# An attention and feed-forward kernel whose engine queues are ordered by a planner: due times in place of keys written by hand, another order of the opening, larger weight pieces, two raw V buffers

## The chip, the cores and the metric

The kernel runs on one core of one Trainium2 chip. The metric is the device time of one execution in microseconds; the time before is 560.06 us, the median of three runs. The work of a core is done by five queues that run beside each other and wait for each other through semaphores: TensorE (PE: matmuls), VectorE (DVE), ScalarE (ACT), GpSimd (POOL), and SyncE (SP), which here issues all loads, transposes and copies by DMA; stores of the output are issued by ScalarE. Each queue is worked off in the order in which the program emits it, so an instruction that waits holds up all that stand behind it on its engine.

## The reference, cut to what matters

```python
# batch, n_heads, seq, head_dim = 8, 8, 576, 64;  d_model 512, d_ff 1024;  stride = 32
scores = scale * np.matmul(q, k.transpose(0, 1, 3, 2))
rel = pos[:, None] - pos[None, :]
mask_local = (rel >= 0) & (rel < stride)                       # heads 0 to 3
mask_strided = (rel >= 0) & (pos[None, :] % stride == pos[:, None] % stride)   # heads 4 to 7
attn = softmax(np.where(masks, scores, -1e9))                  # + 1e-9 in the denominator
x = (attn @ v).transpose(0, 2, 1, 3).reshape(B * S, H * D)     # 4608 x 512

h = x @ w_in
sm = softmax(h)                                                # + 1e-9 in the denominator
solu = h * sm
ln = (solu - mean(solu)) / np.sqrt(var(solu) + 1e-06) * g_ln
out = ln @ w_out
```

Half of the heads attend to the last 32 positions, the other half to positions of the same residue modulo 32. w_in and w_out arrive as float64.

## The kernel before, in words

**Tiling.** Attention is cut into 40 units, five for each of the 8 batches (`UNITS`): two strided units (6 and 5 groups of three residues, 54 positions each) and three local ones (3 blocks of 64 queries against 96 keys). The feed-forward part is cut into 36 tiles of 128 tokens (`ff`). A batch has 4.5 tiles, so one tile in nine lies across the boundary of two batches. The attention output goes to `xhi` and `xlo`, a ring of two batches, split into a high and a low float16 part; the feed-forward part multiplies three pairs (hi hi, hi lo, lo hi) in place of one fp32 product.

**A unit** (`unit`): scores on TensorE with the mask added by a matmul with the unit matrix (lines 342 and 347, into `s_ps`); row maximum and subtraction on VectorE (353, 354), exp on ScalarE (356), row sums and reciprocals on VectorE (357, 361, 362), scaling on GpSimd (365), high part on ScalarE (371) and low part on VectorE (372), a DMA transpose into `pt` (374), the product with V on TensorE (395, called pv, into `x_ps`), and its high and low parts into the ring (411, 412).

**V** (`load_v`, `v_scale`, `v_split`): each batch's V is loaded raw into one pair of buffers, `vrl` (local heads) and `vrs` (strided heads). ScalarE sums its squares (284); a matmul with a matrix of ones adds them over the partitions (249, `pow2_scale`); VectorE makes a power of two of it; V is split into two float16 parts (302, 303), and DMA copies bring them into the layouts `ve` and `vd` (318). The sum of the squares goes into the last column of the second bank of `s_ps`, the tile that the scores also write, and its step comes ahead of unit 0 in the plan.

**Weights** (`decode`, `prep_w`, `prep_o`): float64 values are loaded as pairs of 32-bit words, in 16 pieces of 512 KB (529), into "rooms": `e`, `u` and four `room` tiles for w_in, then `room`, one `ct` tile, `e[1]` and `u[1]` for w_out. ScalarE unpacks the high word (532), VectorE puts in the remaining bits (535, 536). Sums of squares (548, 561) give a scale through `pow2_scale`; then high and low float16 parts are made (553, 554 for w_in; 584, 586, 587 for w_out, after eight matmuls at 571 that subtract the mean over the gains).

**A tile** (`ff`): g1 is 24 matmuls of 512 columns in two halves of one PSUM bank each (453 to 455, into `h_ps`, three banks in turn). VectorE takes the maximum (460), ScalarE the exp (462), VectorE the product u and its sum (464), ScalarE the squares (468), GpSimd the two factors r and f (472 to 485); ScalarE and VectorE write the high and low parts of c = u r (492, 493); a DMA transpose makes `ct` of it (496); g2 is 24 matmuls into `o_ps` (505 to 507); ScalarE scales by f and stores (513). `e`, `u` and `c` have two buffers, `ct` has three. The factors r and f come from one GpSimd step that also needs the scale of w_out.

**What sets the order.** Nothing is issued directly. Each step is added to a `Plan` with its engine, an estimated duration, a function that emits it, a key, and what it reads and writes. `Plan.order` then simulates the five queues with these durations: whenever an engine is free, it takes, of the steps whose inputs are there, the one with the smallest key; the program is emitted in the order in which the simulation starts the steps. Semaphores enforce the dependencies on the chip, so the plan only fixes the order on each queue. The keys are hand-written numbers: `UK` for units, `TK` for tiles, `VK` and `LK` for V and loads, `LF` and `LW` for the first loads and the weights, with offsets within a unit or tile (`key + 0.35`):

```python
UK = [-40.0, -39.5, -39.0, -8.0, -7.0, *(n - 6.0 for n in range(5, B * NU))]
TK = [-6.5, -6.2, -5.9, *(1.11 * t + 1.0 - 2.0 * (t >= NT - 3) for t in range(3, NT))]
...
add("pe", 2.6, lambda i=i: g2(i), key + G2LAG, r=[(*CT, i, 0), (*CT, i, 1), *(("o_w", cc) for cc in range(4 * i, 4 * i + 4))], w=[O])
...
n = min((n for n in ns if ready_at[n] <= now), key=lambda n: (steps[n][3], n))
```

Of the kernel before, what the change touches and what calls it, by code (L numbers as in the profile page):

```python
# [61 lines left out]

class Plan:
# [29 lines left out]

    def order(self):
        steps = self.steps
        left = [len(s[4]) for s in steps]
# [45 lines left out]
def attn_solu_kernel(ctx: ExitStack, tc: tile.TileContext, qloc, qstr, kloc, kstr, vloc, vstr, w_in, w_out, g, masks, out):  # L142
# [67 lines left out]
    add("dve", 0.2, init, -9, w=["nhalf"])  # L210
    add("dve", 0.3, lambda: nc.vector.memset(ones, 1.0), -9, w=["ones"])

    def masks_bf16():
# [1 line left out]
        nc.vector.tensor_copy(mk_loc[:, 0, 0:1], m[:, 0:1])
# [2 lines left out]
        nc.vector.tensor_copy(mk_str, m[:, 2:3, 0:QS].broadcast_to([P, 6, QS]))
# [465 lines left out]
```

## Time and profile before

| | |
|---|---|
| three runs | 557.83, 560.06, 561.62 us; median 560.06 |
| profiled execution | span 558.1 us |
| TensorE busy | 483.2 us, 87% of the span |
| VectorE, ScalarE, GpSimd busy | 367.5, 298.2, 162.7 us |
| DMA | 96.90 MB, 174 GB/s in the mean; read from HBM 39.24 MB, written 9.44 MB |

The span is that of one profiled execution on the chip; the median of the runs lies 2.0 us above it. Engines overlap, so their busy times don't add up to the span. In the slices of the page each digit is the busy share of a fortieth of the span (14 us) in tenths; PEclk is the clock that TensorE was granted, in tenths of the full one. In a line of waits stand who waited, for whom, the total in us, how often, and the longest. In a line of the timeline stand start and duration in us, engine, line, operation, operands and number, and in brackets the idle time before it and what ended it. In a line of a group the number after "x" is the count, then busy us and mean ns of one, then the idle time before.

### The profile page before, as it was taken

Reading aid. Unit: us, or ns where it says so; the run is one execution under the profiler, and the core shown is the slowest. Engines: PE = TensorE matmul, PEld = TensorE weight load, DVE = VectorE, ACT = ScalarE, POOL = GpSimd, SP = SyncE. Lnnn points to the kernel's source line nnn. Section 1 sums busy time; section 2 is a strip of 40 time slices with the busy share of each in tenths; the row PEclk is TensorE's granted clock in tenths of the full one; section 3 lists DMA queues with packets and bytes.
Section 4 is the critical chain, followed back from the end, with each engine's and each line's share of the span. In section 5 each row is a group of like instructions: output and inputs, shape, how many; then the busy total and the mean of one; then the engine's idle time right before and its main releaser. Section 6 shows DMA issues by size and latency. Waiting matters only on the chain.

```text
span 558.1 us, 11783 instructions
## 1 busy us (share of the span) xinstructions
PE 483.2 (87%) x4808; PEld 249.6 (45%) x4808; DVE 367.5 (66%) x647; ACT 298.2 (53%) x440; POOL 162.7 (29%) x306
## 2 busy tenths in 40 slices
PE   0235875798969999999989999999999999999986
PEld 0232452355534555454545555545544554444432
DVE  3499588788865687695757857867566776342440
ACT  3783645375456367455465557546745545344360
POOL 2221004532333242242324332423404323123130
PEclk9999997699988999999999999999999999999999
DMA  8999396569994999599839996798669545542242
GB/s 312 413 282 217 94 213 160 125 135 209 249 210 86 233 254 174 101 230 239 200 66 208 200 252 156 168 275 177 147 95 229 129 96 111 83 95 75 58 111 78
DMA packets 171350, 96.90 MB, mean 174 GB/s; under 512 B 138400, under 2 KB 157472, under 8 KB 171296
## 3 DMA queue, kind: packets, MB, share of 16 engines
q1 hardware_dynamic: 166112, 86.71, 71.3%
q10 hardware_dynamic: 5184, 9.44, 5.3%
q8 instruction: 37, 0.61, 0.5%
q14 instruction: 17, 0.14, 0.1%
HBM read 39.24 MB, written 9.44 MB: 87 GB/s over the span
## 4 chain that ended last, share of the span: by engine, by line
PE 63%; DVE 15%; DMA 8%; ACT 5%; issue 4%; POOL 4%; SPq 0%; ACTq 0%; DVEq 0%; POOLq 0%
PE h_ps L453 10%; PE h_ps L455 9%; PE h_ps L454 9%; PE o_ps L505 8%; PE o_ps L507 7%; PE o_ps L506 7%; DMA vrl<-vloc 4%; PE x_ps L395 3%; PE s_ps L347 3%; DVE u L464 3%; DVE c L493 2%; DVE st L460 2%; DMA pt<-p 2%; PE o_ps L571 1%; DVE m L357 1%
## 5 line engine op out<-in xcount | busy, mean ns | idle before, releaser
L453 PE MATMUL h_ps<-w,xhi 128*128 128x512 f16 x280 | 109.3, 390 | 23.5 <-DVE u L464 18.8
L454 PE MATMUL h_ps<-w,xhi 128*128 128x512 f16 x280 | 109.0, 389 | 0.0
L455 PE MATMUL h_ps<-w,xlo 128*128 128x512 f16 x280 | 108.9, 389 | 0.0
L505 PE MATMUL o_ps<-obuf,ct 128*128 128x512 f16 x272 | 103.5, 381 | 0.8 <-ACT ob L513 0.8
L506 PE MATMUL o_ps<-obuf,ct 128*128 128x512 f16 x272 | 103.2, 379 | 0.0
L507 PE MATMUL o_ps<-obuf,ct 128*128 128x512 f16 x272 | 103.1, 379 | 0.0
L365 POOL TENSOR_TENSOR t<-t,m 128x576 f32<-128x576 f32 (+2 forms) x40 | 51.4, 1284 | 137.0 <-DVE m L362 93.1
L462 ACT ACTIVATE e<-h_ps,st,vsc 128x1024 f32<-128x1024 f32 x31 | 37.3, 1204 | 69.3 <-DVE st L461 51.5
L460 DVE TENSOR_REDUCE st<-h_ps 128x1 f32<-128x1024 f32 x35 | 42.7, 1220 | 43.6 <-PE h_ps L455 43.6
L472 POOL TENSOR_SCALAR st<-st 128x1 f32<-128x1 f32 x36 | 12.9, 358 | 174.7 <-DVE st L467 174.4
L464 DVE SCALAR_TENSOR_TENSOR u<-h_ps,e 128x1024 f32<-128x1024 f32 x35 | 42.7, 1221 | 28.3 <-ACT e L462 17.9
L493 DVE SCALAR_TENSOR_TENSOR c<-u,st,c 128x1024 f16<-128x1024 f32 (+1 forms) x38 | 48.1, 1271 | 13.0 <-ACT c L492 12.9
L492 ACT ACTIVATE c<-u,st 128x1024 f16<-128x1024 f32 (+1 forms) x38 | 41.6, 1100 | 26.3 <-POOL st L482 26.0
L468 ACT ACTIVATE e<-u,st 128x1024 f32<-128x1024 f32 x36 | 41.3, 1147 | 22.8 <-DVE st L467 19.9
L454 PEld LDWEIGHTS <-xhi 128*128 128x128 f16 x288 | 28.6, 99 | 51.9 <-issue 25.0
L455 PEld LDWEIGHTS <-xlo 128*128 128x128 f16 x288 | 28.8, 100 | 36.3 <-issue 3.3
L507 PEld LDWEIGHTS <-ct 128*128 128x128 f16 x288 | 28.2, 98 | 36.7 <-DMA ct<-c 2.9
L453 PEld LDWEIGHTS <-xhi 128*128 128x128 f16 x288 | 28.9, 100 | 33.8 <-issue 2.9
L506 PEld LDWEIGHTS <-ct 128*128 128x128 f16 x288 | 28.3, 98 | 35.2 <-issue 2.7
L505 PEld LDWEIGHTS <-ct 128*128 128x128 f16 x288 | 28.3, 98 | 33.7 <-issue 0.6
L372 DVE TENSOR_TENSOR p<-t,p 128x576 f16<-128x576 f32 (+2 forms) x40 | 30.5, 763 | 16.5 <-ACT p L371 16.2
L347 PE MATMUL s_ps<-k,q 64*54 64x54 f32 (+1 forms) x1280 | 41.1, 270 | 0.0
(132 smaller groups left out, 732.0 us busy)
## 6 DMA issues: line engine op xcount, KB each, us to landing
out<-ob ACTq DMA_DIRECT2D x36, 256.0 KB, 3.2
vrs<-vstr SPq DMA_DIRECT2D x8, 768.0 KB, 5.6
vd<-vs SPq DMA_DIRECT2D x16, 384.0 KB, 8.0
vrl<-vloc SPq DMA_DIRECT2D x8, 640.0 KB, 5.8
q<-qstr SPq DMA_DIRECT2D x8, 594.0 KB, 5.2
k<-kstr SPq DMA_DIRECT2D x8, 594.0 KB, 6.6
q<-qloc SPq DMA_DIRECT2D x8, 576.0 KB, 4.5
k<-kloc SPq DMA_DIRECT2D x8, 576.0 KB, 6.5
```

Of the source, the lines that this page charges most:

```text
L347: nc.tensor.matmul(s_ps[row : row + nq, pair, i * nk : (i + 1) * nk], q_raw[half][hs, q0 : q0 + (nq - 1) * nqb + 1 : nqb], k_raw[half][hs, ...
L365: add("pool", nx * nk / 500 + 0.1, lambda: nc.gpsimd.tensor_tensor(tv, tv, sm.unsqueeze(2).broadcast_to([P, nx, nk]), op=ALU.mult), key + ...
L453: nc.tensor.matmul(hv[:, i], xhi[:, cc, tok], whi[:, cc, cols], start=(cc == 0), stop=False)
L454: nc.tensor.matmul(hv[:, i], xhi[:, cc, tok], wlo[:, cc, cols], start=False, stop=False)
L455: nc.tensor.matmul(hv[:, i], xlo[:, cc, tok], whi[:, cc, cols], start=False, stop=(cc == 3))
L460: add("dve", 1.21, lambda: nc.vector.tensor_reduce(nm, hv, axis=AX.XY, op=ALU.max, negate=True), key + 0.2, r=HH, w=[(ST, "nm")])
L464: add("dve", 1.3, lambda: nc.vector.scalar_tensor_tensor(uv, hv, 1.0, ev, op0=ALU.mult, op1=ALU.mult, accum_out=us), key + 0.3, r=[*HH, E] ...
L492: add("act", w / 1020 + 0.15, lambda cols=cols: nc.scalar.mul(c[:, 0, cols], u[:, cols], r), key + 0.4, r=[U, (ST, "r")], w=CC[0][mine])
L493: add("dve", w / 880 + 0.15, lambda cols=cols: nc.vector.scalar_tensor_tensor(c[:, 1, cols], u[:, cols], r, c[:, 0, cols], op0=ALU.mult, o ...
L505: nc.tensor.matmul(o, ct[:, cc, :], ohi[:, cc, :], start=(cc == 0), stop=False)
L506: nc.tensor.matmul(o, ct[:, cc, :], olo[:, cc, :], start=False, stop=False)
L507: nc.tensor.matmul(o, ct[:, 8 + cc, :], ohi[:, cc, :], start=False, stop=(cc == 7))
```

## The change

**Due times.** The keys are gone. Only three kinds of steps get a date in microseconds: each tile's g1 (`G1`, from 3.59 in steps of 12.74), each tile's g2 (`G2`, 31.30 to 34.52 after g1 for the first seven tiles, then falling to 17.64 for the last; the store 4 later) and each unit's pv (`PV`). `Plan.dues` goes through the steps from last to first and gives every other step the earliest time that its users ask for: the user's due time less its own estimated duration times a slack factor of its engine, less 0.50 a hop, less 5.34 for a DMA's latency, less 6.88 more for a step that depends on nothing. `order` takes the ready step with the smallest due time. (A parameter `dma` of `add` and a set `loads` are read by the planner but never filled.)

**The opening.** For batch 0 the sum of V's squares goes into bank 2 of `h_ps` in place of `s_ps`. The casts of the masks to bf16 move from VectorE to GpSimd, the strided one first. The matrix of ones is bf16, and the sums of squares are read by the matmul as the upper halves of the fp32 values, in all three uses of `pow2_scale`.

**Weights.** w_in comes in four pieces of 1 MB and w_out in four, each into two neighbouring rooms; for that, `e`, `u` and the rooms are one tile `raw`, and `c` and `ct` one tile `cc`. w_in uses all four pairs (`e`, `u`, two of `room`); w_out uses the two pairs of `room`, `ct[1]` with `ct[2]`, and the first pair of `room` again.

**V.** From batch 2 on raw V alternates between the old pair of buffers and a second one that lies in the four rooms; batch 2's load waits until w_out's last steps have left them. `vd` is laid out so that each partition is copied in runs of 1536 elements and not of 256.

**Tiles 0 to 3.** The GpSimd step is cut in two: r first, without the scale of w_out, and f after it. Later tiles keep the old steps.

```diff
-UK = [-40.0, -39.5, -39.0, -8.0, -7.0, *(n - 6.0 for n in range(5, B * NU))]
-TK = [-6.5, -6.2, -5.9, *(1.11 * t + 1.0 - 2.0 * (t >= NT - 3) for t in range(3, NT))]
-G2LAG = 0.55
+FIRST = 3.59
+STEP = 12.74
+LEAD = 18.32
+LAG = [31.30, 34.52, 17.64]
+G1 = [FIRST + STEP * n for n in range(NT)]
+G2 = [G1[n] + (LAG[0] + (LAG[1] - LAG[0]) * n / 6 if n < 6 else LAG[1] + (LAG[2] - LAG[1]) * (n - 6) / (NT - 7)) for n in range(NT)]
+PV = [FIRST - 4.0 + STEP * 0.9 * (n - 2) - LEAD * min(1.0, max(0, n - 2) / 5) for n in range(B * NU)]
...
+    DMA_LATENCY = 5.34
     DMA_AHEAD = 1.0
-    HOP = 0.4
+    HOP = 0.50
+    SLACK = {"pe": 0.89, "act": 1.59, "dve": 1.94, "pool": 0.82, "sp": 0.80}
+    LOAD_LEAD = 6.88
...
+    def dues(self):
+        steps = self.steps
+        due = self.due = [float("inf") if s[3] is None else s[3] for s in steps]
+        for m in range(len(steps) - 1, -1, -1):
+            for d in steps[m][4]:
+                e, dur = steps[d][:2]
+                need = due[m] - dur * self.SLACK[e] - self.HOP
+                if e == "sp":
+                    need -= self.DMA_LATENCY
...
+                if not steps[d][4] or d in self.loads:
+                    need -= self.LOAD_LEAD
+                due[d] = min(due[d], need)
...
-                n = min((n for n in ns if ready_at[n] <= now), key=lambda n: (steps[n][3], n))
+                n = min((n for n in ns if ready_at[n] <= now), key=lambda n: (key[n], n))
...
-    rooms = buf("room", [P, 1024], I32, n=4)
+    (raw_sb,) = buf("raw", [P, 8, 1024], I32)
+    rooms = [raw_sb[:, 4 + i] for i in range(4)]
...
+    more = raw_sb[:, 4:8].rearrange("p a f -> p (a f)").bitcast(F32)
+    vr_sb.append([more[:, 0 : VW[0]], more[:, VW[0] : VW[0] + VW[1]]])
+
+    def raw_v(b):
+        return 0 if b < 2 else (b + 1) % 2
...
-    (vd_sb,) = buf("vd", [P, 2, 6, 2, 4 * D], F16)
+    (vd_sb,) = buf("vd", [P, 2, 2, 6 * 4 * D], F16)
...
-        nc.vector.tensor_copy(mk_str, m[:, 2:3, 0:QS].broadcast_to([P, 6, QS]))
+        nc.gpsimd.tensor_copy(mk_str, m[:, 2:3, 0:QS].broadcast_to([P, 6, QS]))
...
-                nc.tensor.matmul(tot, ones, part, start=(i == 0), stop=(i == len(parts) - 1))
+                nc.tensor.matmul(tot, ones, part.bitcast(BF16)[:, 1:2], start=(i == 0), stop=(i == len(parts) - 1))
...
+        w = [("vr", a, raw_v(b))] + ([("room", i) for i in range(4)] + [("half", i) for i in range(8)] if b == 2 else [])
+        load((1.8, 2.2)[a], vr_sb[raw_v(b)][a], (vloc, vstr)[a][b], w)
...
+        room = (s_ps[:, 1, 511:512], ("s", 1)) if b else (h_ps[:, 2, 0:1], ("h", 2))
...
-        add("pe", nx * (0.063 if half else 0.095) + 0.1, pv, key + 0.9, r=[PT, *VR], w=X)
+        add("pe", nx * (0.063 if half else 0.095) + 0.1, pv, PV[n], r=[PT, *VR], w=X)
...
-            add("pe", 2.6, lambda i=i: g1(i), key, r=[*ring, *(("w", cc) for cc in range(4))], w=[HH[i]])
+            add("pe", 2.6, lambda i=i: g1(i), G1[n], r=[*ring, *(("w", cc) for cc in range(4))], w=[HH[i]])
...
+        if n < EARLY:
+
+            def first():
+                nc.gpsimd.tensor_scalar(t1, mean, mean, TINY, op0=ALU.mult, op1=ALU.add)
+                nc.gpsimd.tensor_scalar(v, sq, 1.0 / DF, t1, op0=ALU.mult, op1=ALU.add)
+                nc.gpsimd.tensor_tensor(r, v, nhalf, op=ALU.pow)
...
+            def second():
+                slope()
+                nc.gpsimd.tensor_scalar(a, sq, o_sc[:, 2:3], z2, op0=ALU.mult, op1=ALU.add)
+                nc.gpsimd.tensor_tensor(ra, a, nhalf, op=ALU.pow)
+                nc.gpsimd.tensor_scalar(f, ra, v, r, op0=ALU.mult, op1=ALU.mult)
...
-            add("pe", 2.6, lambda i=i: g2(i), key + G2LAG, r=[(*CT, i, 0), (*CT, i, 1), *(("o_w", cc) for cc in range(4 * i, 4 * i + 4))], w=[O])
+            add("pe", 2.6, lambda i=i: g2(i), G2[n], r=[(*CT, i, 0), (*CT, i, 1), *(("o_w", cc) for cc in range(4 * i, 4 * i + 4))], w=[O])
...
-    O_ROOMS = ROOMS[4:] + [(ct_sb[2].rearrange("p a f -> p (a f)").bitcast(I32), [("ct", 2, y, a) for y in range(2) for a in range(2)]), ROOMS[2], ROOMS[3], ROOMS[4]]
+    ROOMS = [(raw_sb[:, 2 * i : 2 * i + 2], R) for i, R in enumerate((
+        [("e", 0), ("e", 1)], [("u", 0), ("u", 1)], [("room", 0), ("room", 1)], [("room", 2), ("room", 3)]))]
+    LAST_ROOM = (cc_sb[:, 3:5].bitcast(I32), [*CT[1], *CT[2]])
...
-        add("sp", 1.5, lambda: nc.sync.dma_start(raw, src.rearrange("p (f t) -> p f t", t=2)), LW[n], w=RAW)
+        load(2.9, room, src, RAW)
...
-        for cc in range(8):
-            decode(obuf[:, cc], w_out[cc * P : (cc + 1) * P, :], key, [("od", cc)], O_ROOMS[cc], 8 + cc)
+        for i in range(4):
+            src = w_out[2 * i * P : 2 * (i + 1) * P, :].rearrange("(a p) f -> p a f", p=P)
+            decode(obuf[:, 2 * i : 2 * i + 2].rearrange("p a f -> p (a f)"), src, 4 + i, [("od", 2 * i), ("od", 2 * i + 1)],
+                   (ROOMS[2], ROOMS[3], LAST_ROOM, ROOMS[2])[i])
```

More of the change, by code (lines that the diff above doesn't have):

```diff
@@ L125, in order @@
                 free[e] = max(now + 0.55, dma_free - self.DMA_AHEAD)
+                end = dma_free + self.DMA_LATENCY
+            elif n in self.dma:
+                free[e] = now + dur
+                dma_free = max(dma_free, free[e]) + self.dma[n]
                 end = dma_free + self.DMA_LATENCY
@@ L270, in load_qk @@
+    def load_qk(b, half):
         w = 2 * (S, SP)[half]
         k0 = 0 if half else KPAD
[L272 to L279 removed]
+        load(1.65, q_raw[half][:, 0:w], (qloc, qstr)[half][b], [("q", half)])
+        load(1.65, k_raw[half][:, k0 : k0 + w], (kloc, kstr)[half][b], [("k", half)])
@@ L285, in v_scale @@
-            add("act", (1.25, 1.47)[a], square, key, r=[("vr", a)], w=["junk", ("vm", b % 2, a)])
-        pow2_scale(sc, [vm[:, 0:1], vm[:, 1:2]], key, [("vm", b % 2, a) for a in range(2)], ("vsc", b % 4),
-                   (s_ps[:, 1, 511:512], ("s", 1)), 8, 1.0 / P_SCALE)
+                nc.scalar.activation(junk[:, 0 : VW[a]], vr_sb[raw][a], AF.Square, scale=2.0**-SQ, accum_out=vm[:, a : a + 1])
+            add("act", (1.25, 1.47)[a], square, None, r=[("vr", a, raw)], w=["junk", ("vm", b % 2, a)])
@@ L289, in hscale @@
+        room = (s_ps[:, 1, 511:512], ("s", 1)) if b else (h_ps[:, 2, 0:1], ("h", 2))
+        pow2_scale(sc, [vm[:, 0:1], vm[:, 1:2]], [("vm", b % 2, a) for a in range(2)], ("vsc", b % 4), room, 8, 1.0 / P_SCALE)
         def hscale():
@@ L536, in bits @@
             nc.vector.scalar_tensor_tensor(di, di, 3, w0, op0=ALU.logical_shift_left, op1=ALU.bitwise_or)
-        add("dve", 1.12, bits, key, r=[*RAW, *w], w=[*w, *RAW], lock=True)
-    def prep_w(key):
-        stage = [x.rearrange("p a f -> p (a f)").bitcast(F32) for x in (*c_sb[:2], *ct_sb[:2])]
-        halves = [(y, a) for y in range(2) for a in range(2)]
-        ST = [[(("c", i), *h) for h in halves] for i in range(2)] + [[("ct", i, *h) for h in halves] for i in range(2)]
+        add("dve", 2.12, bits, None, r=[*RAW, *w], w=[*w, *RAW], lock=True)
@@ L544, in prep_w @@
+    def prep_w():
+        stage = [cc_sb[:, i].bitcast(F32) for i in range(4)]
+        ST = [[("c", i, y, a) for y in range(2) for a in range(2)] for i in range(2)] + CT[:2]
         for cc in range(4):
-            for i in range(2):
-                decode(stage[cc][:, i * 512 : i * 512 + 512], w_in[cc * P : (cc + 1) * P, i * 1024 : i * 1024 + 1024],
-                       key, ST[cc][2 * i : 2 * i + 2], ROOMS[2 * cc + i], 2 * cc + i)
+            decode(stage[cc], w_in[cc * P : (cc + 1) * P, :].rearrange("p (a f) -> p a f", a=2), cc, ST[cc], ROOMS[cc])
```

261 lines of the change are left out of this document (133 added, 128 removed).

## The prediction

> **What bounds the kernel now.** I read the page first (its shares and its forty slices), then the busy time in stretches of 20 us, then TensorE's waits, then the timeline of the stretches where those waits lie.
>
> ```profile
> span 558.1 us, 11783 instructions
> PE 483.2 (87%) x4808; PEld 249.6 (45%) x4808; DVE 367.5 (66%) x647; ACT 298.2 (53%) x440; POOL 162.7 (29%) x306
> PE   0235875798969999999989999999999999999986
> PEclk9999997699988999999999999999999999999999
> ```
>
> TensorE (PE) is busy 87% of the span, but not evenly: from the thirteenth slice on nearly every digit is a 9, and all that is missing lies in the first twelve slices, about 167 us, where the granted clock also dips. So there are two stages: a saturated one, which can only get shorter if TensorE's own work shrinks, and an opening.
>
> ```profile
> 0.00:20.00 20.00, 0.00 (x0) 0.00 (x0) 6.64 (x17) 7.57 (x11) 3.62 (x13) 1.00 0.91 344
> 20.00:40.00 20.00, 9.09 (x164) 8.14 (x164) 15.93 (x32) 17.16 (x27) 5.17 (x3) 1.00 1.06 337
> 40.00:60.00 20.00, 8.93 (x129) 5.29 (x130) 16.87 (x26) 9.72 (x17) 3.18 (x2) 1.00 0.97 212
> 60.00:80.00 20.00, 20.00 (x216) 11.47 (x215) 14.81 (x35) 10.00 (x21) 1.15 (x1) 1.00 0.66 133
> 80.00:100.00 20.00, 8.75 (x84) 4.05 (x78) 18.03 (x29) 10.54 (x16) 7.75 (x8) 0.73 0.65 152
> 100.00:120.00 20.00, 19.49 (x169) 9.23 (x169) 14.06 (x26) 12.82 (x19) 9.39 (x17) 0.85 0.63 135
> 120.00:140.00 20.00, 18.39 (x281) 10.66 (x283) 16.86 (x33) 11.31 (x16) 4.88 (x9) 1.00 0.92 196
> 140.00:160.00 20.00, 18.61 (x230) 9.97 (x227) 15.79 (x27) 10.15 (x15) 7.14 (x10) 1.00 1.09 238
> 160.00:180.00 20.00, 16.53 (x136) 7.57 (x133) 10.83 (x26) 12.06 (x18) 5.22 (x14) 0.83 0.63 137
> ```
>
> Columns: busy time of PE, its weight loads, DVE (VectorE), ACT (ScalarE) and POOL (GpSimd), then clock, DMA share and GB/s. In the opening TensorE idles 20.0 + 10.9 + 11.1 us in the first 60 and 11.3 in 80 to 100. The DMA engines are full up to 60 us and VectorE is the busiest compute engine from 20 on (80 to 90%). The waits say what TensorE waited for:
>
> ```profile
> PE s_ps L249 <- ACT junk L284: 21.5, 2, 20.5
> PE h_ps L453 <- DVE u L464: 18.8, 7, 7.7
> PE x_ps L395 <- DMA vd<-vs: 8.0, 2, 7.1
> PE s_ps L342 <- DVE t L354: 5.2, 2, 3.4
> ```
>
> ```profile
> 23.47 0.49 PE L342 MATMUL s_ps<-mk_str,unit 64*64 64x324 bf16 x4 [0.76 <-DVE vsc L255]
> 64.45 0.38 PE L453 MATMUL h_ps<-w,xhi 128*128 128x512 f16 x1
> 64.66 0.38 PE L454 MATMUL h_ps<-w,xhi 128*128 128x512 f16 x1
> 100.51 0.58 PE L453 MATMUL h_ps<-w,xhi 128*128 128x512 f16 x1 [7.68 <-DVE u L464]
> 100.89 0.63 PE L454 MATMUL h_ps<-w,xhi 128*128 128x512 f16 x1
> 101.31 0.63 PE L455 MATMUL h_ps<-w,xlo 128*128 128x512 f16 x1
> 165.77 0.59 PE L453 MATMUL h_ps<-w,xhi 128*128 128x512 f16 x1 [3.47 <-DVE u L464]
> 284.43 0.38 PE L453 MATMUL h_ps<-w,xhi 128*128 128x512 f16 x1 [2.21 <-DVE u L464]
> ```
>
> The first thing on TensorE's queue is the sum of V's squares, and it waits 20.5 us for V; the scores of unit 0 stand behind it and run at 23.47. The first feed-forward matmul (g1 of tile 0) runs at 64.45. After the waits of 7.68 and 3.47 the matmuls come every 0.42 to 0.43 us instead of 0.21, so such a wait costs about 12 x 0.215 = 2.6 us more; after 2.21 they don't.
>
> **The change part by part.** The rows that price the opening:
>
> ```profile
> 1.25 5.13 DMA k<-kstr
> 6.40 12.67 DMA vrl<-vloc
> 49.04 8.94 DMA pt<-p
> ```
>
> ```profile
> 6.74 0.21 DVE L215 CAST mk_loc<-mask 128x96 bf16<-128x96 f32 x1 [5.62 <-DMA mask<-masks]
> 7.40 0.32 DVE L218 CAST mk_str<-mask 128x324 bf16<-128x324 f32 x1
> 27.97 0.42 DVE L535 TENSOR_SCALAR room<-room 128x512 int32<-128x512 int32 x1
> 28.50 0.69 DVE L536 SCALAR_TENSOR_TENSOR ct<-ct,room 128x512 int32<-128x512 int32 x1
> 61.46 0.55 DVE L412 TENSOR_TENSOR xlo<-x_ps,xhi 128x384 f16<-128x384 f32 x1
> ```
>
> ```profile
> L354 DVE TENSOR_TENSOR t<-s_ps,m 128x576 f32<-128x576 f32 (+2 forms) x40 | 30.5, 764 | 1.1
> L412 DVE TENSOR_TENSOR xlo<-x_ps,xhi 128x384 f16<-128x384 f32 (+2 forms) x40 | 25.4, 638 | 18.7 <-ACT xhi L411 18.7
> L554 DVE SCALAR_TENSOR_TENSOR w<-ct,w_sc,w 128x1024 f16<-128x1024 f32 x2 | 2.5, 1274 | 0.0
> L303 DVE SCALAR_TENSOR_TENSOR vs<-vrs,vsc,vs 128x1536 f16<-128x1536 f32 x8 | 14.5, 1814 | 2.1 <-ACT vs L302 2.0
> L566 POOL TENSOR_SCALAR gmat<-g 128x1024 f32<-128x1024 f32 x1 | 2.8, 2802 | 19.0 <-DMA g<-g 19.0
> L249 PE MATMUL s_ps<-vm,ones 128*128 128x1 f32 x32 | 5.1, 259 | 21.5 <-ACT junk L284 21.5
> ```
>
> *First scores ahead of the squares.* The sum for batch 0 gets bank 2 of h_ps, so the scores need only q, k and the strided mask. k lands at 6.38 (1.25 + 5.13) and the mask by 6.74. The mask cast moves to GpSimd, strided first: by L566, 2.74 ns an element, 324 elements take 0.9 us, and by VectorE's 0.32 at the least. First scores then run at 7.1 to 7.7 instead of 23.47. The casts leave VectorE about 1.0 us (6.74 to 7.72) and the local ones, 576 elements, 1.6 us on GpSimd, are hidden: the local units come later. (The Trainium skill, "GPSIMD Engine Reference", section 4.1, has elementwise work with one input at roughly line rate on GpSimd; the 2.80 us of L566 for 1024 elements does not agree, and by the rule the first scores would come half a microsecond sooner, which the sum would not show.)
>
> *Order of the loads.* Due times worked back by hand put the mask and strided q and k first (about -61), then V (-57), local q and k (-40), then the four pieces of w_in. For w_in, as an example: from g1's 3.59, each step's planned duration times its engine's slack and 0.5 a hop are taken off for the low half, high half, scale, sum, squares, bits and unpacking (to -13.7), then 2.3 for the load and 0.5 + 5.34 + 6.88: -29. Before, five of eight w_in pieces went ahead of V, whose last transfer took 12.67 us. By the shapes, mask, q, k and V are 3.9 MB and w_in 4.2 MB: 8.1 MB at 337 to 344 GB/s are 24 us. So w_in is complete at about 24 to 26, hardly later than now (its last piece is unpacked at 27.97), while V, behind 1.3 MB instead of 4, comes some 7 us sooner. SP issues all of these without a wait, so the moved loads hold up nothing behind them.
>
> *1 MB pieces.* The bytes are the same; the number of unpacking steps halves. 512-wide ones cost VectorE 0.42 + 0.69; doubled width saves only the fixed part, which I put at 0.1 us, from 16 x 2 instructions to 8 x 2: 1.6 us of VectorE. A first piece that lands later costs at most one 512 KB transfer, 1.5 us at 344 GB/s, behind which VectorE has scores to work on. (The Trainium skill, "DMA: Bandwidth & Descriptors", section Bandwidth, asks for 1 MiB a transfer and measures 341 GB/s there. The first row of stretches moves 344 GB/s with 512 KB pieces, so the rule's gain is already had: 8.4 MB take 24.4 us by the row and 24.6 by the page.)
>
> *When the first g1 can start.* VectorE has ahead of it: three units at four passes like L354 and one like L412, 3.7 us, with small ones about 4.0: 12.0; w_in 8 x 1.11 = 8.9; its low halves 4 x 1.27 = 5.1; V's low halves, two of at most 1.81: 3.4; scales about 1. That is 30.4, from about 9 us on. Without a gap it ends at 39; at the density of the best 20 us above (18.03 of 20) at 43; at that of 20 to 40 us (15.93) at 47. Now it ends at 62.0 (61.46 + 0.55), because scores start late and w_out's unpacking (due late in the change) is done in between. A queued transpose can still take 8.94 us. I take g1 at 47: 17 us sooner, with 21 and 9 as ends.
>
> *Waits after it.* VectorE's u frees the bank that g1 needs; 18.8 us of waits stand on it, and the clock lost with them is at most 8.1 us (shares 0.27, 0.15 and 0.17 of the 8.75, 19.49 and 16.53 us of busy time). In the change w_out's work ranks behind u by due time, e and u no longer serve as w_out's rooms, and tiles 0 to 3 get their factor r without w_out's scale. But VectorE must still do the same w_out steps and the next units before the second or third tile's g2, so most of these gaps come back elsewhere: I take 4 us of the 27, with 0 and 12 as ends. That the early tiles' GpSimd steps are cut in two costs nothing: as many operations stand behind the squares' sum as before.
>
> *Check on both.* VectorE's busy time up to 160 us is 119.0 (its eight rows above), less 2.6 for the casts and pieces. From 9 us on at 0.80 density it ends at 154, at 0.90 at 138: 6 to 22 us sooner. My 21 is at the dense end, since the loads' wait in the first slice and TensorE's stall at 80 to 100 are what thinned it.
>
> *Sums in bf16.* 56 fp32 matmuls (32 for V at 0.259 us, the rest in w_in's and w_out's scales) become 28 bf16 ones at most; V's 5.1 us falls by between half and all, of which seven eighths lie in the saturated stage: 3 us, ends 2 and 5.
>
> *The rest.* vd in long runs and a second raw V buffer from batch 2 shorten transfers that TensorE rarely waits for once it is saturated: nothing, at most 2 us. The second buffer lies in w_out's rooms, so batch 2's load waits for the last w_out step, and SP's transposes are queued behind it; it costs nothing if SP's order is kept by VectorE, and the length of w_out's delay if not. g2 due 31 to 35 us after its g1, unit dates and all other due times only rearrange a saturated TensorE: nothing, with 0.7 us a tile either way as the bound that the rivals use.
>
> The sum: 558.1 - 17 - 4 - 3 = 534 us of span. The median shown, 560.06, is 2.0 above the profiled span, so **536 us**; with the ends, 518 to 549, and my own working range 522 to 546.
>
> **Rivals.** *The planned dates hold:* g1 at 43, 35 steps of 12.74, then 17.64 to the last g2, 5 for it and 4 to the end: 515, so 517 measured, 506 to 522. For it: nothing in the saturated stage forbids 12.74 a tile. Against it: VectorE would have to be over 90% dense through 100 us. *The DMA engines stay the bound:* the same bytes, with shares 0.91, 1.06 and 0.97 now; V's moves (7.1 us waited) and the 8.94 us transpose then stand behind w_out's and batch 1's loads, which the new order also lets in early. g1 at 55 and no other gain but the sums: 558.1 - 9 - 3 = 546, 548 measured, 546 to 558. *Slower:* in the saturated stage VectorE serves attention steps that are overdue ahead of u, and g1's second half waits for its bank as at 284.43. At 2.21 us for half of 33 tiles that is +36: 572. It decides from 24 / 33 = 0.7 us a tile on. Against it: the stage now has hardly a wait, and the late g2 leaves work between two g1s. For it: the order of every engine is new there, and nothing in the trace shows it.
>
> **How the numbers follow.** Forecast 0.51, planned dates 0.18, DMA bound 0.20, slower 0.11. About 1% (5.6 us) is what a measurement tells from no change, so faster is below 554.5: 0.51 + 0.18 + 0.14 of the DMA case + 0.01 = 0.84; within 1%: 0.06 of the DMA case and 0.01 of the last = 0.07; slower 0.09. The range 508 to 556 leaves out the slower rival, some of the DMA case's top and the lowest dates: about 0.18.
>
> **What would show it.** First scores before 9 us, w_in unpacked by 28, g1 near 47 (55: the DMA rival; 43: the dates), the 20.5 us wait gone, waits of h_ps on u in the opening below 15 us, L249 below 3 us, and a saturated stage without new waits. The prediction is wrong if g1 starts after 58 or if a wait repeats with every tile.

## The result, and the profile after

The changed kernel takes 538.05 us (median of four runs, 536.48 to 539.2) against 560.84 us of the kernel before on the same chip: a ratio of 0.9593, 95% interval 0.954 to 0.9645. The profiled span went from 558.1 to 536.3 us, 21.8 us less. Where one of a kernel's runs was a slow one, its ratio leaves that run out and its median counts it.

The page of the changed kernel, the lines that answer to the first ones quoted of before:

```profile
span 536.3 us, 11679 instructions
...
PE 473.2 (88%) x4780; PEld 242.5 (45%) x4780; DVE 363.0 (68%) x627; ACT 298.4 (56%) x432; POOL 172.1 (32%) x314
...
PE   2027848899999999998999999999999999999994
...
PEclk9998888799999999999999999999999999999999
```

TensorE's busy time fell by 10.0 us, which is less than half of the gain; the rest is idle time. The digits reach 9 in the ninth slice and stay there but for one 8 and the last slice, where before they wavered up to the twelfth. The busy time in stretches (the same columns):

```profile
0.00:20.00 20.00, 3.72 (x98) 3.03 (x98) 9.48 (x18) 11.26 (x12) 7.56 (x18) 1.00 0.91 367
20.00:40.00 20.00, 3.03 (x60) 2.42 (x60) 16.21 (x26) 13.63 (x21) 2.49 (x1) 1.00 1.08 256
40.00:60.00 20.00, 14.13 (x182) 7.64 (x183) 16.97 (x25) 13.86 (x26) 4.90 (x4) 0.87 1.10 318
60.00:80.00 20.00, 11.96 (x174) 6.78 (x176) 17.37 (x35) 11.29 (x18) 2.42 (x2) 0.84 0.80 182
80.00:100.00 20.00, 16.03 (x173) 8.41 (x167) 15.30 (x28) 8.52 (x12) 8.65 (x5) 0.76 0.59 121
100.00:120.00 20.00, 18.86 (x177) 9.33 (x175) 13.39 (x33) 13.22 (x20) 10.18 (x23) 0.93 1.01 178
120.00:140.00 20.00, 20.00 (x210) 10.47 (x209) 17.01 (x29) 13.16 (x20) 10.55 (x17) 1.00 1.02 270
140.00:160.00 20.00, 20.00 (x254) 10.48 (x252) 15.27 (x24) 12.50 (x18) 4.80 (x10) 1.00 1.08 220
160.00:180.00 20.00, 19.87 (x185) 9.98 (x187) 13.07 (x28) 13.05 (x18) 8.71 (x16) 1.00 0.70 172
```

From 120 us on TensorE is full and its clock is 1.00. In the kernel before, 120 to 180 still lacked 6.5 us and the clock was 0.83 in the last 20. Ahead of 100 us the idle time has hardly changed, 51.1 us after 53.2 (the five rows' 20 less busy time, summed); it has only moved, out of the first row, of 40 to 60 and of 80 to 100 into 20 to 40 and 60 to 80. TensorE's waits over the whole span, and the places where the largest of them lie:

```profile
PE s_ps L381 <- DVE t L393: 33.9, 5, 14.2
PE s_ps L381 <- POOL mk_str L249: 4.9, 1, 4.9
...
PE h_ps L492 <- DVE raw L503: 1.2, 1, 1.2
```

```profile
7.12 1.51 PE L386 MATMUL s_ps<-k,q 64*54 64x54 f32 x48 [1.77 <-DMA k<-kstr]
...
26.50 0.45 PE L381 MATMUL s_ps<-mk_loc,unit 64*64 64x288 bf16 x4 [14.18 <-DVE t L393]
...
35.99 0.45 PE L381 MATMUL s_ps<-mk_loc,unit 64*64 64x288 bf16 x4 [7.88 <-DVE t L393]
...
65.18 0.39 PE L492 MATMUL h_ps<-w,xhi 128*128 128x512 f16 x1
...
79.26 0.46 PE L381 MATMUL s_ps<-mk_loc,unit 64*64 64x288 bf16 x4 [8.04 <-DVE t L393]
```

The wait for V is gone and the first scores run at 7.12. In its place stand waits of the next scores on VectorE's t, 14.18, 7.88 and 8.04 us among them: 33.9 us in all. The waits of g1 on u (L464 before, L503 now) fell from 18.8 us in seven to 1.2 us in one. **The first g1 starts at 65.18, no earlier than before (64.45).** This is one half of the tile, 12 matmuls; the next 12 of g1 follow at 67.78, before not until 73.98.

To see where the 21.8 us come from I counted in the timeline how many matmuls TensorE had done by 180 us, and priced them by their spacing in the saturated stage of the changed kernel (after 200 us: 600 of g1 in 133.9 us, 624 of g2 in 140.5, 808 of scores in 25.9, 980 of pv in 20.1). The last column is the time from 180 to the last matmul, less the matmuls that were left; it is negative where the spacing is tighter than these prices. The numbers are good to about 1 us: counted by the start of every matmul they come out up to 1.1 us different.

| kernel | first g1 | done by 180 | lost after 180 |
|---|---|---|---|
| before | 64.5 | 94.9 | 2.0 |
| changed | 65.2 | 110.6 | -4.3 |
| due times alone | 62.9 | 115.4 | 1.5 |
| all but the due times | 57.2 | 110.4 | 16.4 |
| scores first alone | 63.2 | 98.6 | 7.4 |
| sums in fp32 | 66.2 | 109.2 | 4.4 |
| g2 early on TensorE's queue | 65.2 | 110.9 | 9.5 |
| g2 early in the others' dates | 57.3 | 112.2 | 0.2 |
| w_out loaded to an eighth | 58.7 | 117.2 | -2.1 |
| w_out behind w_in's scale | 61.8 | 113.6 | -5.0 |

So 15.7 us of the gain were made by 180 us, with the first g1 where it was, and 6.3 us after it. Of the 15.7, TensorE's idle time gives 7.8 (60.2 and 52.4 us in the nine rows), and the shorter sums of squares 5.1 (6.8 us before and 1.7 now, of those that ran by 180). About 3 us are left: the matmuls come closer together than before, though the clock of the rows is as low.

### The profile page after: what moved, and what is told of

It is laid out like the page before. It is cut to its first block, busy times and chain, and to the rows that moved or that the text cites. A ratio compares the mean times of both kernels' runs of the same rounds, so it can differ in the third digit from the quotient of the medians.

```text
span 536.3 us, 11679 instructions
## 1 busy us (share of the span) xinstructions
PE 473.2 (88%) x4780; PEld 242.5 (45%) x4780; DVE 363.0 (68%) x627; ACT 298.4 (56%) x432; POOL 172.1 (32%) x314
## 4 chain that ended last, share of the span: by engine, by line
PE 73%; DMA 13%; DVE 7%; POOL 2%; issue 2%; ACT 2%; SPq 1%; ACTq 0%; POOLq 0%; DVEq 0%
PE h_ps L492 10%; PE o_ps L565 10%; PE h_ps L493 10%; PE h_ps L494 10%; PE o_ps L567 10%; PE o_ps L566 10%; DMA cc<-cc 7%; PE x_ps L434 5%; PE s_ps L386 4%; DMA raw<-w_out 3%; DMA pt<-p 2%; DMA vrs<-vstr 1%; PE s_ps L381 1%; PE o_ps L632 1%; DVE st L499 1%
## 5 line engine op out<-in xcount | busy, mean ns | idle before, releaser
L492 PE MATMUL h_ps<-w,xhi 128*128 128x512 f16 x280 | 108.0, 386 | 1.3 <-DVE raw L503 1.2
L493 PE MATMUL h_ps<-w,xhi 128*128 128x512 f16 x280 | 107.9, 385 | 0.0
L565 PE MATMUL o_ps<-obuf,cc 128*128 128x512 f16 x272 | 103.4, 380 | 3.6 <-DMA cc<-cc 3.6
L566 PE MATMUL o_ps<-obuf,cc 128*128 128x512 f16 x272 | 103.1, 379 | 0.0
L567 PE MATMUL o_ps<-obuf,cc 128*128 128x512 f16 x272 | 103.1, 379 | 0.0
L404 POOL TENSOR_TENSOR t<-t,m 128x576 f32<-128x576 f32 (+2 forms) x40 | 54.7, 1368 | 92.8 <-DVE m L401 34.9
L553 DVE SCALAR_TENSOR_TENSOR cc<-raw,st,cc 128x1024 f16<-128x1024 f32 (+1 forms) x38 | 48.9, 1290 | 17.5 <-ACT cc L552 17.5
L501 ACT ACTIVATE raw<-h_ps,st,vsc 128x1024 f32<-128x1024 f32 x31 | 37.3, 1203 | 39.5 <-DVE st L500 39.1
L552 ACT ACTIVATE cc<-raw,st 128x1024 f16<-128x1024 f32 (+1 forms) x38 | 41.6, 1100 | 23.9 <-POOL st L542 19.7
L507 ACT ACTIVATE raw<-raw,st 128x1024 f32<-128x1024 f32 x36 | 41.3, 1147 | 18.8 <-DVE st L506 12.9
L411 DVE TENSOR_TENSOR p<-t,p 128x576 f16<-128x576 f32 (+2 forms) x40 | 30.4, 759 | 25.2 <-ACT p L410 25.2
L503 DVE SCALAR_TENSOR_TENSOR raw<-h_ps,raw 128x1024 f32<-128x1024 f32 x35 | 42.5, 1215 | 6.3 <-ACT raw L501 6.3
L567 PEld LDWEIGHTS <-cc 128*128 128x128 f16 x288 | 28.1, 98 | 37.1 <-DMA cc<-cc 3.2
L565 PEld LDWEIGHTS <-cc 128*128 128x128 f16 x288 | 28.1, 97 | 36.7 <-DMA cc<-cc 4.9
L573 ACT ACTIVATE ob<-o_ps,st 128x512 f32<-128x512 f32 x34 | 23.3, 684 | 35.3 <-PE o_ps L567 30.8
```

The costliest lines, as they stand in the source:

```text
L404: add("pool", nx * nk / 500 + 0.1, lambda: nc.gpsimd.tensor_tensor(tv, tv, sm.unsqueeze(2).broadcast_to([P, nx, nk]), op=ALU.mult), None, ...
L492: nc.tensor.matmul(hv[:, i], xhi[:, cc, tok], whi[:, cc, cols], start=(cc == 0), stop=False)
L493: nc.tensor.matmul(hv[:, i], xhi[:, cc, tok], wlo[:, cc, cols], start=False, stop=False)
L503: add("dve", 1.3, lambda: nc.vector.scalar_tensor_tensor(uv, hv, 1.0, ev, op0=ALU.mult, op1=ALU.mult, accum_out=us), None, r=[*HH, E], w=[ ...
L552: add("act", w / 1020 + 0.15, lambda cols=cols: nc.scalar.mul(c[:, 0, cols], u[:, cols], r), None, r=[U, (ST, "r")], w=CC[0][mine])
L553: add("dve", w / 880 + 0.15, lambda cols=cols: nc.vector.scalar_tensor_tensor(c[:, 1, cols], u[:, cols], r, c[:, 0, cols], op0=ALU.mult, o ...
```

## The experiments

**Which half of the change does it.** First the due times alone: the kernel before with the new planner, dates and constants, none of the other edits.

```diff
-            add("pe", 2.6, lambda i=i: g1(i), key, r=[...], w=[HH[i]])
+            add("pe", 2.6, lambda i=i: g1(i), key, r=[...], w=[HH[i]], due=G1[n])
```

> The kernel before with the new planner alone: due times from the dates of g1, g2 and pv, new hop, latency and slack; buffers, pieces of 512 KB, fp32 sums, one raw V buffer and the place of the first sum stay as before. Theory A (the order on the queues is what shortened the stretch from 65 to 176 us: the waits of g1 on u went because VectorE serves u in time): 540 to 548 us. Theory B (the new buffers and the freed first scores did it, the dates only rearrange): 556 to 562 us, with waits of h_ps on u of 15 us or more in the opening as before.

Measured: 540.55 us, ratio 0.9677 (0.9617 to 0.9738). By the ratios that is 18 of the 22.8 us. Then the reverse, the changed kernel with the hand-written keys of before on every step (the lines that hand the keys to the steps are left out here):

```diff
-        key = self.due
+        key = [s[3] for s in steps]
```

> The changed kernel with the hand-written keys of before in place of the due times; everything else of the change stays (first sum in h_ps, masks on GpSimd, bf16 sums, 1 MB pieces, two raw V buffers, vd in long runs, r without w_out's scale in tiles 0 to 3). Theory A (order): 550 to 558 us, only the bf16 sums and some of the early gaps won. Theory B (buffers): 538 to 544 us.

Measured: 559.63 us, ratio 1.001 (0.9982 to 1.0037), above both expectations: all the other edits together bring nothing at the end. The table shows that this isn't because they do nothing. By 180 us this kernel is as far as the changed one (110.4 and 110.6), with its first g1 at 57.2; it loses the lead afterwards. Its waits from 180 on (line 498 is g1, 509 its u):

```profile
PE h_ps L498 <- DVE raw L509: 8.3, 6, 4.2
PE x_ps L440 <- DVE xlo L457: 3.5, 2, 2.7
...
```

In the changed kernel no wait of g1 is left there. The two halves are therefore no sum: by 180 us the dates alone are 20.5 us ahead of the kernel before and the other edits alone 15.5, and what the keys then lose, the dates keep.

**The first scores.** The edit of the bank alone, in the kernel before, and then the changed kernel with this edit taken back:

```diff
-                   (s_ps[:, 1, 511:512], ("s", 1)), 8, 1.0 / P_SCALE)
+                   (s_ps[:, 1, 511:512], ("s", 1)) if b else (h_ps[:, 2, 0:1], ("h", 2)), 8, 1.0 / P_SCALE)
```

> The kernel before with one edit: the sum of V's squares of batch 0 goes into bank 2 of h_ps, so that the first scores need not wait for it. Theory A (the start of g1 is set by the loads, V's moves and the transposes, not by the scores): scores before 10 us, first g1 within 4 us of 64.45, time 557 to 562 us. Theory B (the prediction's: scores 16 us sooner bring g1 forward): first g1 before 58 and 548 to 554 us.

> The changed kernel with that one edit taken back: the sum of batch 0 shares s_ps with the scores again; the planner may shift other steps for it. V now lands at 10.4 us, so the scores should wait until about 13 and not 7 us. Theory A (g1's start is set by loads and transposes): 536 to 540 us. Theory B (the scores carry the opening): 542 to 546 us.

Measured: 556.2 us alone, ratio 0.9944 (0.9904 to 0.9984); 537.03 us with it taken back, 0.959 (0.954 to 0.9639). Early scores are worth 3 us where V comes late, between the two expectations (557 to 562 and 548 to 554). They are worth nothing to be seen where the due times load V early; there the scores started at 8.90 without the edit, not at the 13 that was expected. The row of the first of these kernels in the table is of an execution of 561.03 us, its slowest, so the 7.4 us in it are more than its median lost.

**Sums, pieces, raw V.** The first two go with a second measurement of the changed kernel on the same chip, 538.54 us, ratio 0.9645 (0.9602 to 0.9688).

```diff
-                nc.tensor.matmul(tot, ones, part.bitcast(BF16)[:, 1:2], start=(i == 0), stop=(i == len(parts) - 1))
+                nc.tensor.matmul(tot, ones, part, start=(i == 0), stop=(i == len(parts) - 1))
```

> The changed kernel with the matrix of ones and the squares in fp32 again. By the groups of the kernel before, V's sums cost 5.1 us of TensorE in all, most of it in the saturated stage. Prediction's term: 2 to 5 us slower, 540 to 543. Rival (the sums hide in gaps between matmuls): within 1 us of the changed kernel.

Measured: 545.09 us, ratio 0.9733 (0.9678 to 0.9787), 5 to 6 us more than the changed kernel (4.9 by the ratios), above both expectations. The groups of these sums, first of the changed kernel, then with fp32:

```profile
L284 PE MATMUL s_ps<-vm,ones 128*128 128x1 bf16 x14 | 1.5, 165 | 2.6 <-ACT junk L323 2.6
L284 PE MATMUL h_ps<-o_sc,ones 128*128 128x1 bf16 x8 | 0.4, 165 | 0.0
L284 PE MATMUL h_ps<-vm,ones 128*128 128x1 bf16 x2 | 0.4, 176 | 0.2 <-ACT junk L323 0.2
L284 PE MATMUL h_ps<-w_sc,ones 128*128 128x1 bf16 x4 | 0.3, 171 | 0.0
```

```profile
L284 PE MATMUL s_ps<-vm,ones 128*128 128x1 f32 x28 | 4.0, 242 | 1.6 <-ACT junk L323 1.6
...
L284 PE MATMUL h_ps<-o_sc,ones 128*128 128x1 f32 x16 | 1.9, 251 | 0.0
L284 PE MATMUL h_ps<-w_sc,ones 128*128 128x1 f32 x8 | 1.9, 354 | 0.0
L284 PE MATMUL h_ps<-vm,ones 128*128 128x1 f32 x4 | 1.0, 357 | 0.0
```

In all 2.6 and 8.8 us: the 6.2 us of busy time are about what the end moved by, but they are not in the place where it moved. Some 5 of them lie ahead of 180 us, where this kernel is about 1 us behind by the table. Behind 180 the sums take 1.2 us more (2.0 and 0.8), and there it loses some 8 us. Most of these are clock: in 300 to 340, 420 to 460 and 500 to 540 TensorE was granted 0.96, 0.96 and 0.91, which takes 6.3 of its 112.2 us of busy time there, against 0.9 in the changed kernel (1.00, 1.00 and 0.97); ahead of the last two tiles g2 waited up to 3.0 us for a transpose of c (`cc`), against 1.7. Whether these waits come from the longer sums is not shown.

```diff
-        load(2.9, room, src, RAW)
+        def halves():
+            for a in range(2):
+                nc.sync.dma_start(room[:, a], src[:, a])
+        add("sp", 2.9, halves, None, w=RAW)
```

> The changed kernel with each 1 MB load of weights issued as two transfers of 512 KB (8 more DMAs on the queue); the unpacking steps stay at 1024 columns, the plan is unchanged. Theory A (bytes set the time): within 1 us of the changed kernel. Theory B (each DMA on SyncE's queue waits for the one issued eight before it, so more and smaller ones let later work in later): the first transpose after 33 us where it is issued at 30.8 now, and 2 to 6 us slower.

Measured: 536.92 us, ratio 0.962 (0.9579 to 0.9661). That the time is the same was expected if the bytes set it; the first transpose was issued at 29.5, not after 33 as the other expectation had it. The size of a piece makes no difference that could be seen.

```diff
     def raw_v(b):
-        return 0 if b < 2 else (b + 1) % 2
+        return 0
...
-        w = [("vr", a, raw_v(b))] + ([("room", i) for i in range(4)] + [("half", i) for i in range(8)] if b == 2 else [])
+        w = [("vr", a, raw_v(b))]
```

> The changed kernel with one raw V buffer in place of two; everything else as changed. Theory (TensorE is saturated when batches 2 to 7 load V, as the prediction had it): no difference, 536 to 541 us beside the 538 of the changed kernel. Rival (the second buffer is what lets the squares and splits of a batch run ahead): TensorE waits for moves of V, vd<-vs or ve<-vl, at the starts of batches 2 to 7, about 1 us each, 544 us or more.

Measured: 541.05 us, ratio 0.9617 (0.9559 to 0.9675), which overlaps both intervals of the changed kernel. No effect of the second buffer is shown; one of up to 3 us would not be seen.

**Which of the due times.** A g2 is dated 18 to 35 us after its g1. This date does two things: it places g2 on TensorE's queue, and it sets the dates of all that leads to g2. One kernel keeps the dates of the others and ranks g2 half a step after its g1 on TensorE's queue alone; the other does the reverse.

```diff
+EARLY_G2 = [y + STEP / 2 for y in G1]
...
-        key = self.due
+        key = [self.g2.get(n, y) for n, y in enumerate(self.due)]
...
+            plan.g2[len(plan.steps)] = EARLY_G2[n]
             add("pe", 2.6, lambda i=i: g2(i), G2[n], ...
```

> The changed kernel, but on TensorE's queue alone each tile's g2 ranks half a step (6.37 us) after its g1 in place of 18 to 35 us after it; the due times of all other steps are worked back from the late dates as before. Theory A (the late g2 on TensorE's queue is the gain: it keeps finished g2 work in stock for the time in which VectorE makes u): the waits of h_ps on u come back after 180 us, 8 to 17 us in all, and the time is 546 to 556 us. Theory B (the gain is in what VectorE, ScalarE, GpSimd and SyncE serve first): 536 to 541 us, hardly a wait on u.

> The reverse: TensorE's queue ranks g2 by the late dates of the change, but the due times of all steps that lead to a g2 (softmax, c, transposes, w_out's preparation) are worked back from a date half a step after g1. Theory A: 535 to 542 us, no more waits than in the changed kernel. Theory B: attention steps now come behind all tile steps on VectorE and ScalarE, scores and transposes are late, TensorE waits for them, 546 us or more. In both, w_out's preparation comes earlier in the opening, and the first g1 not before 65 us.

Measured: 552.22 us, ratio 0.9825 (0.9765 to 0.9885), with g2 early on TensorE's queue; 540.23 us, ratio 0.963 (0.9592 to 0.9669), with g2 early for the others alone. So it is the place of g2 on TensorE's queue: 13 to 14 of the 22.8 us are given back when its rank there alone is changed (13.0 by the ratios, 14.2 by the medians, which are of two chips). Stretches of 40 us, first with the early g2, then of the changed kernel:

```profile
380.00:420.00 40.00, 36.29 (x384) 18.52 (x382) 28.55 (x57) 21.95 (x32) 12.63 (x26) 0.91 0.61 143
420.00:460.00 40.00, 37.63 (x368) 19.04 (x367) 23.21 (x36) 17.55 (x27) 12.81 (x23) 1.00 0.59 123
460.00:500.00 40.00, 38.06 (x333) 18.35 (x332) 20.25 (x33) 17.90 (x27) 11.19 (x23) 1.00 0.47 97
```

```profile
380.00:420.00 40.00, 40.00 (x449) 20.88 (x447) 30.28 (x55) 21.73 (x30) 15.60 (x27) 1.00 0.62 116
420.00:460.00 40.00, 39.01 (x390) 19.86 (x383) 27.56 (x44) 20.89 (x31) 11.37 (x24) 1.00 0.68 143
460.00:500.00 40.00, 40.00 (x308) 19.01 (x306) 20.17 (x32) 17.13 (x26) 8.89 (x24) 1.00 0.45 93
```

The busy time differs by 7.0 us here (112.0 and 119.0), and a clock of 0.91 takes another 3.3 of 36.29. Of the waits that were expected on u alone, 8 to 17 us, only 3.5 came on u after 180 and 2.6 more on the maximum before it; the rest is spread over scores and pv. The mechanism that I had in mind, stock for the time in which u is made, is thus part of it, not all: a g2 that is held back is stock against every wait. By 180 both kernels stand equal (110.9 and 110.6).

The reverse kernel starts its first g1 at 57.3 and ends its first g2 19 us earlier than the changed one (92.2 and 111.5), while its first g1 was expected not before 65; by 180 us it is only 1.6 us ahead. The lead was order, not work.

**What holds the first g1.** The changed kernel with the same order, in which three of w_out's loads bring an eighth of their columns:

```diff
-        load(2.9, room, src, RAW)
+        load(2.9, room[:, :, 0:128] if n in (4, 5, 7) else room, src[:, :, 0:128] if n in (4, 5, 7) else src, RAW)
```

> The changed kernel, same order on every queue, but three of the four loads of w_out bring only the first eighth of their columns, 2.75 MB less of the 4.2 MB; so the rest of w_out is not what the reference has. It asks what keeps the first g1 at 65 us. If it is the full DMA engines (at 340 GB/s the 2.75 MB are 8.1 us): the wait for w_out of 14.5 us from 16.2 on and the 10.3 us of transposes at 44 shrink, the first g1 starts at 52 to 58 us, and the time is 526 to 533 us. If it is the order of VectorE's and TensorE's queues (w_out's unpacking and the eight matmuls over the gains stand ahead of the last low halves of w_in and the last product with V): g1 starts at 62 to 66 us and the time is 535 to 539 us.

Measured: 533.78 us, ratio 0.9509 (0.9445 to 0.9574), which lies between the two expectations, and so does the first g1:

```profile
58.71 0.39 PE L492 MATMUL h_ps<-w,xhi 128*128 128x512 f16 x1
```

```profile
20.00:40.00 20.00, 6.98 (x111) 4.79 (x112) 19.31 (x29) 16.18 (x25) 5.00 (x3) 1.00 1.08 292
40.00:60.00 20.00, 15.55 (x230) 8.38 (x229) 19.34 (x37) 14.46 (x27) 2.58 (x2) 0.91 0.65 181
```

From 40 to 60 the DMA share is 0.65 in place of 1.10, and VectorE is full: 38.7 of 40 us. In six profiles of kernels that open like the changed one the first g1 lies between 64.3 and 66.2, so at most about 1 of the 6.5 us is chance. The bytes of w_out thus hold the first g1 back by some 6 us, on the DMA engines themselves or through the waits that hang on their landing, which this run does not separate; behind them stands VectorE, without a gap to fill.

**A version that beats both.** In the plan alone, w_out's loads wait for w_in's scale. That keeps them back, and since a step inherits the dates of those that follow it, w_in's first pieces move ahead of q and k; on the chip nothing new is waited for.

```diff
-        load(2.9, room, src, RAW)
+        load(2.9, room, src, RAW, () if n < 4 else ["w_sc"])
```

> The changed kernel with one more dependency in the plan alone: w_out's loads are planned after w_in's scale, so that the first transpose is issued ahead of the first load of w_out, and VectorE's queue has no w_out piece ahead of w_in's scale. Theory A (w_out's first piece, in front of the first transpose and of VectorE's w_in scale, holds g1 back): first g1 before 58 us where it is at 65.2 now; what the time gains is what w_out's later arrival doesn't take back: 530 to 538. Theory B (the DMA engines' bytes or VectorE's total set g1): first g1 within 3 us of 65, time 537 to 543.

Measured: 533.67 us, ratio 0.9558 (0.9513 to 0.9602), 4.9 us below the changed kernel on the same chip.

```profile
61.82 0.38 PE L492 MATMUL h_ps<-w,xhi 128*128 128x512 f16 x1
```

The time is as expected if w_out's first piece held g1 back, but the first g1 comes only 3.4 us earlier than at 65.18, in neither expectation; 3.0 us more are done by 180. w_in's scale stands at 24.8 in place of 33.7 and its low halves are done at 44.7 in place of 57.8, 13 us sooner; but g1 still comes right behind the sum of w_out's squares, which runs at 61.60.

## Why the prediction was right, and where it was wrong

The time was right (536 against 538.05), and the opening's gain was about there: 17 + 4 us were forecast for it and 15.7 found by 180 us. The way there was not, so the total is in good part luck.

*First scores ahead of the squares:* right, 7.12 against 7.1 to 7.7. The cast of the strided mask on GpSimd:

```profile
4.36 0.46 POOL L249 CAST mk_str<-mask 128x324 bf16<-128x324 f32 x1
```

0.46 us for 324 elements, 1.4 ns each, against the 2.74 of L566, and near VectorE's 0.32. (Here the trace agrees with the Trainium skill, "GPSIMD Engine Reference", section 4.1, elementwise work with one input at roughly line rate, and not with the row that I preferred; the scores waited for k anyway.)

*Order of the loads, 1 MB pieces:* right in its times. w_in's last bits are done at 25.1, and V's sum stands on TensorE at 11.8. But w_in's pieces went ahead of the local q and k (3.60 and 5.88), not behind them: the planner dates them -54.7 to -51.5, not -29, because w_out's pieces want two of w_in's rooms and the buffer of its last piece. Doubled width saved 0.15 us an instruction, not 0.1 (0.42 and 0.69 us at 512 columns, 0.69 and 1.23 at 1024). Halving the pieces changes nothing that could be seen. (By the Trainium skill, "DMA: Bandwidth & Descriptors", section Bandwidth, a transfer should be at least 1 MiB; no gain over 512 KB is to be seen here, 538.54 and 536.92 us.)

***When the first g1 can start* is the step that failed:** 0 us instead of 17. I listed 30.4 us of work for VectorE from 9 us on, at a density of 0.80, with w_out's unpacking "due late in the change". What VectorE did in the changed kernel between 8.6 us and the first g1, in one stretch and in its largest groups:

```profile
8.60:65.20 56.60, 24.11 (x384) 14.51 (x381) 45.19 (x73) 38.88 (x60) 11.19 (x6) 0.94 1.04 299
```

```profile
L596 DVE TENSOR_SCALAR raw<-raw 128x1024 int32<-128x1024 int32 x7 | 5.9, 842 | 2.8 <-DMA raw<-w_out 2.8
L612 DVE SCALAR_TENSOR_TENSOR w<-cc,w_sc,w 128x1024 f16<-128x1024 f32 x4 | 5.0, 1273 | 0.0
...
L393 DVE TENSOR_TENSOR t<-s_ps,m 128x576 f32<-128x576 f32 (+2 forms) x6 | 4.6, 768 | 0.1
L392 DVE TENSOR_REDUCE m<-s_ps 128x6 f32<-128x576 f32 (+2 forms) x6 | 4.5, 755 | 9.1 <-PE s_ps L386 9.1
...
L597 DVE SCALAR_TENSOR_TENSOR obuf<-obuf,raw 128x1024 int32<-128x1024 int32 x3 | 3.7, 1229 | 0.7 <-ACT obuf L593 0.5
...
L597 DVE SCALAR_TENSOR_TENSOR obuf<-obuf,cc 128x1024 int32<-128x1024 int32 x1 | 2.0, 1976 | 0.1
```

45.2 us at a density of 45.19 / 56.6 = 0.80. The density was right; the list was short. All of w_out's unpacking is in what VectorE did (the two groups that write obuf, 5.7 us, and four of the eight shifts of L596, about 3), and six units' maxima and differences where I counted three. 30.4 us at 0.80 end at 47; 45.2 end at 65. In six kernels whose first g1 lies anywhere between 57 and 65, VectorE has 41 to 46 us of work ahead of it.

w_out's unpacking was not "due late", and the code says why: the sum of w_out's squares goes into bank 1 of `h_ps` (line 640, and 579 before), and the second half of tile 0's g1 writes the same bank, so by the plan it has to follow all of w_out's loading, unpacking and squares. Worked back from there by the planner of the changed kernel, w_out's four unpacking steps are due at -22.4 to -7.4, three of w_in's four low halves (L612) only at -0.9, and w_out's sum at 0.1 stands ahead of g1, at 2.0, on TensorE's queue. The trace has this order:

```profile
30.71 0.70 DVE L596 TENSOR_SCALAR raw<-raw 128x1024 int32<-128x1024 int32 x1 [2.81 <-DMA raw<-w_out]
33.67 0.15 DVE L290 TENSOR_SCALAR w_sc<-h_ps 128x1 int32<-128x1 int32 x1
51.93 1.98 DVE L597 SCALAR_TENSOR_TENSOR obuf<-obuf,cc 128x1024 int32<-128x1024 int32 x1
55.28 2.47 DVE L612 SCALAR_TENSOR_TENSOR w<-cc,w_sc,w 128x1024 f16<-128x1024 f32 x2
```

```profile
58.82 4.24 PE L632 MATMUL o_ps<-obuf,gmat 128*128 128x512 f32 x6
63.68 0.35 PE L284 MATMUL h_ps<-o_sc,ones 128*128 128x1 bf16 x8
```

The first piece of w_out even stands ahead of w_in's scale on VectorE: in the simulation it was ready first, on the chip its load landed at 30.7, and the scale, whose sum had run on TensorE at 28, waited until 33.7. That much the kernel with w_out behind w_in's scale mends. No run puts w_out's sum into another bank, so what its place costs is not measured; that VectorE's list as a whole set the 65 is in part argued, since it also had 11.4 us of gaps, and w_out's bytes held some 6 us of it.

*Waits after it:* "most of these gaps come back elsewhere" was right. g1's waits on u fell by 17.6 us (18.8 to 1.2), but 10.0 of the scores' 33.9 us of waits lie behind the first g1 (8.04 at 79.26, 1.98 at 93.53), and TensorE's idle time from the first g1 to 180 us fell from 18.2 to 13.3 us, by 4.9 where the term had 4. With the 3 us that are left over above, which also fall in the opening, it is at most about 8, inside the ends of 0 and 12. The lost clock stayed by the rows: with 0.87, 0.84, 0.76 and 0.93 it takes 8.9 us between 40 and 120, after 8.1 before.

*Sums in bf16:* mis-sized, 5 to 6 us when taken back, not 3 (ends 2 and 5), and the mechanism is not shown. I let V's 5.1 us alone fall and forgot that the sums for w_in's and w_out's scales fall with them: 8.9 us before (5.1, and 3.8 of the scales), 2.6 after. Nor do seven eighths of V's sums lie in the saturated stage: half of the 32 had run by 180. What the fp32 sums lose behind 180 is more than their own time there.

*The rest:* "g2 due 31 to 35 us after its g1, unit dates and all other due times only rearrange a saturated TensorE: nothing" is the second step that failed. Against a rank half a step after g1, the late g2 alone is worth 13 to 14 us, 0.4 us a tile, inside the bound of 0.7 that I gave and then set to nothing. Against the kernel before it brings less, 6.3 us after 180, since that kernel's keys lost only 2.0 there. The second raw V buffer: nothing to be seen, to within 3 us; the long runs of vd were not tried by themselves. Two smaller slips: from 20 to 40 us ScalarE (17.16) and not VectorE (15.93) was the busiest engine, and the low end of the sum, 518, is one of the span, 520 as a measured time.

*The rivals.* The DMA engines as the bound: half there, some 6 us of the first g1's delay go with w_out's bytes, with g1 even later than the 55 of that rival; but its "no other gain but the sums" was wrong. The planned dates: the first g1 lies 22 us behind them, and from the fifth g2's end (161.4) to the 28th (451.1) a tile takes 289.7 / 23 = 12.6 us, so their step of 12.74 holds. The slower one did not come: one wait of g1 on u in the whole span. By my own sign, "wrong if g1 starts after 58", the prediction was wrong; the total came out because terms that I had set low made up for the 17 us: idle time ahead of the first g1 gave about 3, what follows it up to 180 at most 8 in place of 4, the sums about 6 of TensorE's time in place of 3, and the stage behind 180 about 5 more, where nothing was forecast.

What stays open: why the order alone is further by 180 us (115.4) than with the other edits (110.6), and why these alone reach the same 110.4. VectorE's busy time up to there (129.8 us before, 134.1 changed, 142.0 and 141.7 in the two halves) shows no common ceiling.

## What to carry to other kernels

When an engine is nearly full, ask what it holds in stock: a step that is ready and can be put off, such as the second product of a tile, is worth more behind the work that others wait for than right after its inputs, and it costs nothing to try. Before you call work late, follow its outputs to the first thing that needs them: one shared bank made all of w_out urgent here. And a planner that takes what its simulation holds for ready can put late data ahead of urgent work, as w_out's first piece was put ahead of w_in's scale. Check a forecast at a point half way, here the work done by 180 us, not only at the end, where errors of both signs cancel.

## What the runs showed of the hardware

What SyncE issued in the opening of the changed kernel, and one of its waits:

```profile
16.20 0.39 SPq L305 DMA_DIRECT2D raw<-w_out  x1
...
30.77 5.22 SPq L413 DMA_TRANSPOSE pt<-p  x1
...
44.48 10.34 SPq L413 DMA_TRANSPOSE pt<-p  x2
...
58.50 1.43 SPq L413 DMA_TRANSPOSE pt<-p  x1
```

```profile
SPq L413 <- DMA raw<-w_out: 6.3, 1, 6.3
```

The softmax of unit 0 was complete at 25.8, yet its transpose was issued at 30.77, as soon as w_out's first piece (issued at 16.20) had landed. In the trace none of this queue's 196 DMAs starts before the one that was issued eight before it has landed, and w_out's piece was the eighth before the transpose. A large load can so hold a small urgent transfer that has nothing to do with it. And an issue isn't free: this transpose kept SyncE 5.22 us and the next two 10.34, one at 58.50 only 1.43. The DMA share was 1.08, 1.09 and 1.01 in these three stretches, so full DMA engines alone do not make the difference; what does is not shown. None of the runs separates these two costs from the order of the queue.
